# Forward segment in another order: V before Q and among turns and scores, out-projection in two parts

## The chip, the cores and the metric

One NeuronCore of a Trainium2 chip. The metric is the device time of one execution in microseconds (us). Runs of the kernel before took 2990.2, 2992.72 and 2992.77 us, median 2992.72 us. The traces come from one further execution of each kernel under the hardware profiler.

## The reference

A transformer block with a recurrent memory, and its gradients. The change touches the forward attention alone:

```python
B, S, Dm = (1, 2048, 512)
H, Dh = (32, 128)
M, seg = (8, 32)
...
for s in range(n_seg):
    xs = x[:, s * seg_len:(s + 1) * seg_len, :].copy()
    h = jnp.concatenate([mem, xs], axis=1)
    q = jnp.einsum('btd,dhe->bhte', h, Wq)
    k = jnp.einsum('btd,dhe->bhte', h, Wk)
    v = jnp.einsum('btd,dhe->bhte', h, Wv)
    scores = jnp.einsum('bhqe,bhke->bhqk', q, k) * scale
    scores = jnp.where(mask[None, None], scores, -1000000000.0)
    p = _softmax(scores, axis=-1)
    o = jnp.einsum('bhqk,bhke->bhqe', p, v)
    o = jnp.einsum('bhte,hed->btd', o, Wo)
    mem = o[:, :M, :].copy()
    outs.append(o[:, M:, :])
```

There are 64 segments of 32 rows. Each takes the 8 memory rows that the segment before put out, so 40 rows stand in front of the projections and the segments run strictly one after the other. Around this the reference has a layernorm with conditioning, a gated feed-forward block, and the gradients of all weights; those stages are the same in both kernels.

## The kernel before

The forward is `phase2`, a Python loop `for s in range(NS)` that writes out 64 segments. `pin` then fixes each engine's instructions in the order in which the program states them, so the source order is the order of every engine. Four segments make a tile of 128 rows; `s4 = s % 4` is a segment's place in it.

A segment does the following, in this order. The names are those of the profile.

- K and Q: `proj` calls `col_pass` (L257), 32 columns of TensorE at a time, four such column groups side by side, two halves for each of K and Q. VectorE copies the first half from PSUM to `RA`, ScalarE the second. `RA` holds heads in rows of four.
- V in three chunks: `v_chunk` (L673), twice 512 columns and once 384, again in 32-column groups. The first two carry rows of the tile after (`hb`, the last 8 rows of each segment) in the fourth group. Their copies go to `Vst` and `RBv`.
- Turns (`turns`, L851): eight 128x128 transposes each of k and q, and copies by `to_heads` into `kT` (ScalarE) and `qT` (VectorE). `to_heads` has an own part (three of four heads, in two halves of 4) and a far part (the heads of the fourth row group, two instructions).
- Scores (`st_exp`, L861) in three parts of 4, 4 and 3 head groups, each group three heads of 40 rows, then an exp on ScalarE into `ET`.
- Column sums (`den`, L867), reciprocals on VectorE, products with V (`pv`, L887) into `or_ps`, and `ost`, which scales the result into `Ost`: parts 0 and 2 on VectorE (L911), part 1 on ScalarE in four instructions.
- Turns of O (`ott`, through `transposes_part`, L879) and copies into `OT`.
- Out-projection (`outproj`, `pair_mm` L223): 16 pairs of heads, each four matmuls of 32 columns, all into one PSUM tile `at_ps`.
- The fold: `split_pair` makes a high part (ScalarE `at_hi`) and a low part (VectorE `at_lo`), `sum_pair` adds them on TensorE (`at_ft`, L242), and ScalarE writes the new memory rows into the `hT` of the next segment (L1058), for which its K waits.

Other work stands between these: `p1` is the layernorm of a later tile in five steps (0 load of x on SP's queue, 1 statistics, 2 scaling, 3 shift and a store by POOL, 4 turn on TensorE); `fill` issues pieces of the next tile's last-8-rows projections and turns (`b_pieces`); `tail.chunk` the out-projection of such rows (L215); `pop_later` a postponed fold or turn of rows that go to DRAM. The queue of SP (SyncE) carries the loads and stores in program order: stores of `RA` (`rows_out`), two transposing transfers (`VTr` from `Vst`, `Pst` from `ET`), stores of `Ost` and `OT`. POOL multiplies `Pst` by the reciprocals (L1076, in `norm`), copies the last-8-row columns into `kT` and `qT` (`tails_in`), and issues the transfers of `v_tails`.

PSUM tiles of the forward come from one pool of 5 buffers with the tag "p" and one of 3 for the scores; a new tile waits until the buffer that it gets has been read out.

```python
                    v_chunk(s, 0)
                    turns()
                    v_chunk(s, 1)
...
                st_exp(0)
                st_exp(1)
                st_exp(2)
```

Of the kernel before, what the change touches and what calls it, by code (L numbers as in the profile page):

```python
# [40 lines left out]
class K:  # L41
# [403 lines left out]
    def phase2(self):  # L445
# [15 lines left out]
        with ExitStack() as ctx:  # L461
# [234 lines left out]
            def v_chunk(s, k):  # L696
# [4 lines left out]
                ps = psp.tile([128, 512], F32, name="pass_ps", tag="p")  # L701
                hT = get_ht(s)
                for c in range(DC):
# [4 lines left out]
                if k > 0:  # L708
                    v_evac(("dve", "act")[k - 1], Vsts[s % 2], ps, a, n)
                for hl, ta, tn, o in tails_of:  # L710
                    self.evac(("act", "dve")[k], RBv[(t + 1) % 2][32 * hl:32 * hl + 32, ta * E:(ta + tn) * E],
                              ps[96:128, o * E:(o + tn) * E])
                if k == 0:
                    v_evac("dve", Vsts[s % 2], ps, a, n)
# [109 lines left out]
            for s in range(NS):  # L824
                s4 = s % nseg_t
                if s4 == 0:
                    if s > 0:
                        p1(s // nseg_t + P1_AHEAD, 0)
# [18 lines left out]
                def turns(xs=(("k", "act"), ("q", "dve"))):  # L847
                    for x, eng in xs:
                        tp = psp.tile([128, 8, 128], BF16, name="turn_ps", tag="p")
                        for i in range(8):  # L850
                            nc.tensor.transpose(tp[:, i, :], RA[x][:, i * 128:i * 128 + 128], self.ident[:, :])  # L851
                        for hf in range(2):
                            to_heads(eng, XT[x], tp[:, 4 * hf:4 * hf + 4, :], 4 * hf, 4, 32, 0, far=False)
                        to_heads(eng, XT[x], tp[:], 0, 8, 32, 0, own=False)

                def st_exp(pi):
                    st_ps = masked.pop(pi)
                    n = min(PG, G - pi * PG)
                    for j in range(n):
                        g = pi * PG + j  # L860
                        nc.tensor.matmul(st_ps[:, j, 0:120], lhsT=x120(KT, g), rhs=QT[:, g * 120:g * 120 + 120],  # L861
# [52 lines left out]
                def ott(pi):  # L914
                    ps, n = transposes_part(Ost, pi, m=120)
                    self.evac("dve" if pi == 0 else "act", part3(OT, pi)[:, 0:n, 0:120], ps)

                def outproj():
                    ps = psp.tile([128, 256], F32, name="at_ps", tag="p")
                    off = lambda h: (h // 3) * GW + (h % 3) * 32  # L920
                    order = [*range(12, 16), *range(8, 12), *range(8)] if s == 0 else range(H // 2)
                    for n, p in enumerate(order):
                        hs = (2 * p, 2 * p + 1)
# [17 lines left out]
                if s == 0:  # L941
# [6 lines left out]
                    turns((("k", "act"),))  # L948
# [1495 lines left out]
```

## Time and profile before

| | before |
|---|---|
| median of the runs shown | 2992.72 us |
| the profiled execution | 2989.77 us |
| its span, first to last instruction | 2988.0 us |
| TensorE matmul busy | 2907.6 us, 97% |
| VectorE / ScalarE / POOL busy | 55% / 45% / 41% |
| forward: first K matmul of segments 0 and 63 | 18.3 us, 950.0 us |
| granted TensorE clock | 0.996 |

The span is the time from the first to the last instruction of one execution. Busy TensorE is not TensorE at its peak: a matmul's record includes its passage through the array, and records overlap. In lists in order of time the first column is the start and the second the duration of the merged row in us; then engine, line, operation, the tile written and the tiles read, shape, and how many instructions were merged. What stands in brackets is idle time ahead of the row and what ended it. "PE" is TensorE, "PEld" its weight load, "DVE" VectorE, "ACT" ScalarE.

### The profile page before, as it was taken

The page shows a single profiled execution, that of the slowest core. Times are in us where ns is not written, and L with a number is a line of the kernel's source. Part 1 is how long each engine was busy: PE and PEld are TensorE (multiplying, and loading weights), DVE is VectorE, ACT ScalarE, POOL GpSimd, SP SyncE. Part 2 cuts the span into 40 slices and gives each one's busy share as a digit, 9 for nine tenths or more (in the row PEclk, how much of TensorE's full clock was granted, in tenths as well). Part 3 has the DMA queues.
Part 4 walks back from the last instruction along what each step waited for, and adds up shares of the span by engine and source line. Part 5 has one row for each costly group of instructions (what it writes and reads, how often), then busy time and mean ns, then how long its engine had stood idle before and what let it go on. Part 6 is the DMA issues. An engine that isn't in the chain of part 4 may idle for free.

```text
span 2988.0 us, 105331 instructions
## 1 busy us (share of the span) xinstructions
PE 2907.6 (97%) x43742; PEld 1825.2 (61%) x43816; DVE 1639.3 (55%) x3680; ACT 1347.5 (45%) x3244; POOL 1228.8 (41%) x2485
## 2 busy tenths in 40 slices
PE   6999999999999999999999999999999999999999
PEld 3666666666666544446567777777777754445455
DVE  5566656666655788833356666656566632850011
ACT  3666666666666533312355555555555520110011
POOL 2455555544555222221244444444444422762111
PEclk8999999999999999999999999999999999999999
DMA  9998988888889899988699999999999997886565
GB/s 308 212 229 216 214 210 225 205 218 216 211 217 267 219 232 231 232 274 284 191 256 255 250 256 246 257 253 252 251 247 252 246 283 246 252 262 191 159 216 171
DMA packets 837922, 703.01 MB, mean 235 GB/s; under 512 B 537682, under 2 KB 709890, under 8 KB 836548
## 3 DMA queue, kind: packets, MB, share of 16 engines
q1 hardware_dynamic: 711828, 485.29, 65.9%
q0 software_dynamic: 54512, 148.63, 15.8%
q10 hardware_dynamic: 71104, 62.34, 6.5%
q8 instruction: 345, 5.65, 0.8%
q14 instruction: 133, 1.09, 0.1%
HBM read 294.99 MB, written 276.35 MB: 191 GB/s over the span
## 4 chain that ended last, share of the span: by engine, by line
PE 68%; DMA 2%; DVE 1%; ACT 1%; issue 1%; POOL 0%; SPq 0%; DVEq 0%; ACTq 0%; POOLq 0%
PE gps L2225 14%; PE dh_ps L215 8%; PE pass_ps L257 7%; PE g_ps L1848 5%; PE gps5o L2240 4%; PE dhq_ps L223 4%; PE mm L1329 3%; PE dh_tps L215 3%; PE gps L1508 3%; PE mm L1289 2%; PE mm L1304 2%; PE tps L1765 2%; PE mm L1258 1%; PE mm L1262 1%; PE turn_ps L1721 1%; PE gps L1407 1%
## 5 line engine op out<-in xcount | busy, mean ns | idle before, releaser
L2225 PE MATMUL gps<-rows,hrows 128*128 128x512 bf16 (+2 forms) x2124 | 413.6, 355 | 1.9
L2225 PEld LDWEIGHTS <-hrows 128*128 128x128 bf16 x2160 | 211.1, 98 | 204.5 <-issue 0.9
L63 DVE CAST ot<-gps 128x512 bf16<-128x512 f32 (+3 forms) x76 | 48.2, 634 | 309.2 <-PE gps L2225 229.1
L1076 POOL TENSOR_TENSOR Pst<-Pst,rden 120x1408 bf16<-120x1408 bf16 x63 | 159.7, 2536 | 132.4 <-issue 84.2
L61 ACT ACTIVATE ot<-gps 128x512 bf16<-128x512 f32 (+3 forms) x75 | 41.2, 549 | 349.5 <-PE gps L2225 214.8
L1893 POOL COPY dOst<-RAd 96x512 bf16<-96x512 bf16 x128 | 75.3, 611 | 298.7 <-DVE RAd L63 298.5
L673 PE MATMUL pass_ps<-Wv,hT 128*32 128x512 bf16 (+2 forms) x2304 | 186.7, 358 | 0.0
L2229 POOL DMA_DIRECT2D out_dram<-ot x104 | 78.5, 755 | 254.8 <-DVE ot L63 129.2
L257 PEld LDWEIGHTS <-hT 128*32 128x32 bf16 x4096 | 114.7, 97 | 98.5 <-issue 4.4
L223 PE MATMUL at_ps<-Wo,OT 128*32 128x256 bf16 x4096 | 125.9, 276 | 10.6 <-ACT OT L61 5.5
L215 PE MATMUL dh_ps<-WvT,dVT 128*32 128x512 bf16 x2048 | 134.0, 381 | 1.6
L63 DVE CAST Vst<-pass_ps 96x512 bf16<-96x512 f32 x128 | 87.2, 682 | 84.8 <-ACT RBv L61 76.2
L673 PE MATMUL pass_ps<-Wv,hb 128*32 128x512 bf16 (+2 forms) x636 | 127.5, 348 | 2.1 <-DMA Wv<-in_A_Wv_dram 2.1
L257 PE MATMUL pass_ps<-Wk,hT 128*32 128x512 bf16 x2048 | 123.4, 382 | 2.5 <-DVE mv L402 1.1
L257 PE MATMUL pass_ps<-WoT,dyT 128*32 128x256 bf16 (+1 forms) x3072 | 122.5, 308 | 1.1 <-ACT dyT L1974 0.9
L223 PE MATMUL dhq_ps<-WqT,dQT 128*32 128x256 bf16 x4096 | 123.1, 273 | 0.0
L257 PE MATMUL pass_ps<-Wq,hT 128*32 128x512 bf16 x2048 | 122.7, 379 | 0.0
L215 PE MATMUL dh_ps<-WkT,dKT 128*32 128x512 bf16 x2048 | 122.3, 380 | 0.0
L2240 PE MATMUL gps5o<-WoT,rows 128*128 128x512 bf16 x549 | 120.4, 379 | 0.6
L223 PEld LDWEIGHTS <-OT 128*32 128x32 bf16 x4096 | 107.8, 97 | 21.4 <-issue 12.7
L814 POOL DMA_DIRECT2D Vst<-RBv x192 | 100.3, 527 | 48.5 <-ACT ET L863 31.2
L223 PEld LDWEIGHTS <-dQT 128*32 128x32 bf16 x4096 | 109.8, 97 | 15.9 <-issue 0.2
(473 smaller groups left out, 6989.4 us busy)
## 6 DMA issues: line engine op xcount, KB each, us to landing
OSR<-Ost SPq DMA_DIRECT2D x64, 352.0 KB
OT<-OT SPq DMA_DIRECT2D x64, 352.0 KB
PS<-Pst SPq DMA_DIRECT2D x64, 352.0 KB
Pst_l<-PS SPq DMA_DIRECT2D x64, 352.0 KB
OT_l<-OT SPq DMA_DIRECT2D x64, 352.0 KB
DVR<-rows_x POOLq DMA_DIRECT2D x64, 352.0 KB, 6.3
DKR<-rows_x POOLq DMA_DIRECT2D x64, 352.0 KB, 5.8
DQR<-rows_x POOLq DMA_DIRECT2D x64, 352.0 KB, 3.2
```

The lines of the kernel that those rows point to most:

```text
L63: return nc.vector.tensor_copy(out, in_)
L215: self.nc.tensor.matmul(ps[32 * j:32 * j + 32, :], lhsT=lhsT, rhs=w, start=(n < 4), stop=(n >= total - 4), tile_position=(0, 32 * j))
L223: nc.tensor.matmul(ps[32 * j:32 * j + 32, :], lhsT=x[k], rhs=w[k][:, 256 * d:256 * d + 256], start=(n == 0), stop=(n == total - 1), tile_p ...
L257: self.nc.tensor.matmul(ps[32 * j:32 * j + 32, :], lhsT=lhs(c), rhs=rhs, start=(c == 0), stop=(c == DC - 1), tile_position=(0, 32 * j))
L673: nc.tensor.matmul(ps[32 * j:32 * j + 32, o * E:(o + n) * E], lhsT=lhsT, rhs=wc[:, 3 * a + hl:3 * (a + n - 1) + hl + 1:3, :], start=(c == ...
L814: nc.gpsimd.dma_start(Vst[96 + 8 * j:104 + 8 * j, :], rb[32 * j + o:32 * j + o + 8, :])
L1076: nc.gpsimd.tensor_tensor(Pst[0:120, :, :], Pst[0:120, :, :], rden[:, :].unsqueeze(2).to_broadcast([120, G, 128]), op=ALU.mult)
L1329: nc.tensor.matmul(hp[:], lhsT=xT[:, fc, :], rhs=wT[:, fc, :], start=(n == 0), stop=(n == 2 * FC - 1))
L1508: nc.tensor.matmul(ps[:], lhsT=h2r[:, j, c * 128:(c + 1) * 128], rhs=xr[:, j, :], start=(j == 0), stop=(j == NT - 1))
L1848: nc.tensor.matmul(ps[:, j, 0:w], lhsT=lh[:, g * GW:(g + 1) * GW], rhs=rh[:, g * GW:g * GW + w], start=True, stop=True)
L2225: nc.tensor.matmul(ps[:, 0:ng * E], lhsT=hrows[:, tp_, c * 128:(c + 1) * 128], rhs=rows[:, tp_, 0:ng * E], start=(tp_ == 0), stop=(tp_ == ...
L2240: nc.tensor.matmul(pss[gg][:], lhsT=rows[:, t, gg * E:(gg + 1) * E], rhs=dyrows[:, t, :], start=(n == 0), stop=(n == NTP - 1))
```

## The change

K is followed by V's first chunk, then Q. The turns of q come in two halves, and V's second chunk in two halves by rows of the contraction (`v_products` with `cs`), so that the order on TensorE is: turns of k, first half of q's turns, half of V1, second half of q's turns, scores part 0, rest of V1, scores part 1, half of V2, scores part 2, rest of V2. The copies stand in the order in which the scores need them, and k's far copies go from ScalarE to VectorE. The last score group of parts 0 and 1 reads 120 columns of `KT` in place of 128. Ahead of the last part of `pv` stand the fill of turns and `p1` step 4. The turn of O's part 0 and its copy come before the last `ost`; parts 1 and 2 share one PSUM tile, and part 2's copy goes from ScalarE to VectorE. The first 6 pairs of the out-projection run between the turns of parts 1 and 2. The steps of `p1` are spread over other segments (load and statistics at s4 = 2, scaling at s4 = 3, shift at s4 = 0, turn at s4 = 1).

```diff
--- before.py
+++ after.py
@@ -693,25 +693,31 @@
                             v_mm(ps, j, c, hb_rows(0)(c), j, a, n)
                     v_evac("dve", RBv[0], ps, a, n)
 
-            def v_chunk(s, k):
+            def v_products(s, k, ps, cs):
 
                 t, s4 = s // nseg_t, s % nseg_t
                 a, n = VCH[k]
                 tails_of = VTAILS.get((s4, k), ()) if t + 1 < NT else ()
-                ps = psp.tile([128, 512], F32, name="pass_ps", tag="p")
+                ps = ps or psp.tile([128, 512], F32, name="pass_ps", tag="p")
                 hT = get_ht(s)
-                for c in range(DC):
+                for c in cs:
                     for j in range(3):
                         v_mm(ps, j, c, hT[:, c, :], j, a, n)
                     for of in tails_of:
                         v_mm(ps, 3, c, hb_rows(t + 1)(c), *of)
-                if k > 0:
-                    v_evac(("dve", "act")[k - 1], Vsts[s % 2], ps, a, n)
-                for hl, ta, tn, o in tails_of:
+                return ps
+
+            def v_copies(s, k, ps):
+
+                t, s4 = s // nseg_t, s % nseg_t
+                a, n = VCH[k]
+                v_evac(("dve", "dve", "act")[k], Vsts[s % 2], ps, a, n)
+                for hl, ta, tn, o in VTAILS.get((s4, k), ()) if t + 1 < NT else ():
                     self.evac(("act", "dve")[k], RBv[(t + 1) % 2][32 * hl:32 * hl + 32, ta * E:(ta + tn) * E],
                               ps[96:128, o * E:(o + tn) * E])
-                if k == 0:
-                    v_evac("dve", Vsts[s % 2], ps, a, n)
+
+            def v_chunk(s, k):
+                v_copies(s, k, v_products(s, k, None, range(DC)))
 
             def fill(s4, where):
                 for f in slots.pop((s4, where), []):
@@ -823,9 +829,9 @@
 
             for s in range(NS):
                 s4 = s % nseg_t
+                if s4 == 2:
+                    p1(s // nseg_t + P1_AHEAD + 1, 0)
                 if s4 == 0:
-                    if s > 0:
-                        p1(s // nseg_t + P1_AHEAD, 0)
                     slots = b_pieces(s // nseg_t + 1) if s + nseg_t < NS else {}
                 hT = get_ht(s)
                 hT_next = get_ht(s + 1) if s + 1 < NS else None
@@ -844,21 +850,31 @@
                     for x in "kq":
                         rows_out(RA[x], DR[x], s, 1)
 
-                def turns(xs=(("k", "act"), ("q", "dve"))):
-                    for x, eng in xs:
-                        tp = psp.tile([128, 8, 128], BF16, name="turn_ps", tag="p")
-                        for i in range(8):
-                            nc.tensor.transpose(tp[:, i, :], RA[x][:, i * 128:i * 128 + 128], self.ident[:, :])
-                        for hf in range(2):
-                            to_heads(eng, XT[x], tp[:, 4 * hf:4 * hf + 4, :], 4 * hf, 4, 32, 0, far=False)
-                        to_heads(eng, XT[x], tp[:], 0, 8, 32, 0, own=False)
+                def turn_mm(x, tp, hf):
+                    tp = tp or psp.tile([128, 8, 128], BF16, name="turn_ps", tag="p")
+                    for i in range(4 * hf, 4 * hf + 4):
+                        nc.tensor.transpose(tp[:, i, :], RA[x][:, i * 128:i * 128 + 128], self.ident[:, :])
+                    return tp
+
+                def turn_own(x, tp, hf, eng):
+                    to_heads(eng, XT[x], tp[:, 4 * hf:4 * hf + 4, :], 4 * hf, 4, 32, 0, far=False)
+
+                def turn_far(x, tp, eng):
+                    to_heads(eng, XT[x], tp[:], 0, 8, 32, 0, own=False)
+
+                def turns(x, eng):
+                    tp = turn_mm(x, turn_mm(x, None, 0), 1)
+                    turn_own(x, tp, 0, eng)
+                    turn_own(x, tp, 1, eng)
+                    turn_far(x, tp, eng)
 
                 def st_exp(pi):
                     st_ps = masked.pop(pi)
                     n = min(PG, G - pi * PG)
                     for j in range(n):
                         g = pi * PG + j
-                        nc.tensor.matmul(st_ps[:, j, 0:120], lhsT=x120(KT, g), rhs=QT[:, g * 120:g * 120 + 120],
+                        w = 120 if g in (PG - 1, 2 * PG - 1) else 128
+                        nc.tensor.matmul(st_ps[0:w, j, 0:120], lhsT=KT[:, g * 120:g * 120 + w], rhs=QT[:, g * 120:g * 120 + 120],
                                          start=False, stop=True, skip_group_check=True)
                     nc.scalar.activation(part3(ET, pi)[:, 0:n, 0:120], st_ps[:, 0:n, 0:120], AF.Exp, scale=cfg.scale)
 
@@ -911,16 +927,29 @@
                     nc.vector.tensor_tensor(part3(Ost, pi)[0:120, 0:n, :], or_ps[0:120, 0:n, :],
                                             rden[:, pi * PG:pi * PG + n].unsqueeze(2).to_broadcast([120, n, 128]), op=ALU.mult)
 
-                def ott(pi):
-                    ps, n = transposes_part(Ost, pi, m=120)
-                    self.evac("dve" if pi == 0 else "act", part3(OT, pi)[:, 0:n, 0:120], ps)
-
-                def outproj():
-                    ps = psp.tile([128, 256], F32, name="at_ps", tag="p")
+                def ott_first():
+                    ps, n = transposes_part(Ost, 0, m=120)
+                    self.evac("dve", part3(OT, 0)[:, 0:n, 0:120], ps)
+
+                def ott_rest():
+                    ps = psp.tile([128, 2 * PG, GW], BF16, name="tps", tag="p")
+                    for pi in (1, 2):
+                        n = min(PG, G - pi * PG)
+                        for j in range(n):
+                            g = pi * PG + j
+                            nc.tensor.transpose(ps[:, g - PG, 0:120], Ost[0:120, g * GW:(g + 1) * GW],
+                                                self.ident[0:120, 0:120])
+                        self.evac(("act", "dve")[pi - 1], part3(OT, pi)[:, 0:n, 0:120], ps[:, (pi - 1) * PG:(pi - 1) * PG + n, 0:120])
+                        if pi == 1:
+                            yield
+                    yield
+
+                def outproj(ps, a, b):
+                    ps = ps or psp.tile([128, 256], F32, name="at_ps", tag="p")
                     off = lambda h: (h // 3) * GW + (h % 3) * 32
                     order = [*range(12, 16), *range(8, 12), *range(8)] if s == 0 else range(H // 2)
-                    for n, p in enumerate(order):
-                        hs = (2 * p, 2 * p + 1)
+                    for n in range(a, b):
+                        hs = (2 * order[n], 2 * order[n] + 1)
                         self.pair_mm(ps, [OT[:, off(h):off(h) + 32] for h in hs], [Wo[:, h, :] for h in hs], n, H // 2)
                     return ps
 
@@ -945,7 +974,7 @@
                     load_wo(0)
                     for f in firsts["k"]:
                         f()
-                    turns((("k", "act"),))
+                    turns("k", "act")
                     evac_turned()
                     tails_in("k", 0)
                     p1(1, 4)
@@ -960,36 +989,46 @@
                         firsts["q"][hf]()
                         proj("q", hf, ("dve", "act")[hf])
                     firsts["q"][2]()
-                    turns((("q", "dve"),))
+                    turns("q", "dve")
                     evac_turned()
                     tails_in("q", 0)
                     for f in first_stores:
                         f()
                 else:
+                    v_chunk(s, 0)
                     proj("q", 0, "dve")
-                    if s4 == 1:
-                        p1(s // nseg_t + P1_AHEAD, 2)
                     proj("q", 1, "act")
                 if s == NS - 1:
                     first_tile[4]()
                 if s > 0:
-                    v_chunk(s, 0)
-                    turns()
-                    v_chunk(s, 1)
+                    tk = turn_mm("k", turn_mm("k", None, 0), 1)
+                    tq = turn_mm("q", None, 0)
+                    turn_own("k", tk, 0, "act")
+                    turn_own("k", tk, 1, "act")
+                    turn_own("q", tq, 0, "dve")
+                    v1 = v_products(s, 1, None, range(0, DC // 2))
+                    turn_mm("q", tq, 1)
+                    turn_own("q", tq, 1, "dve")
+                    turn_far("k", tk, "dve")
+                    turn_far("q", tq, "dve")
+                st_exp(0)
+                if s > 0:
+                    v_products(s, 1, v1, range(DC // 2, DC))
+                    v_copies(s, 1, v1)
+                st_exp(1)
+                if s > 0:
+                    v2 = v_products(s, 2, None, range(0, DC // 2))
+                st_exp(2)
+                if s > 0:
+                    v_products(s, 2, v2, range(DC // 2, DC))
+                    v_copies(s, 2, v2)
                 if s == NS - 1:
-                    v_chunk(s, 2)
                     first_tile[5]()
-                if s == NS - 1:
                     late_rows()
                     self.glu_first = {1: self.glu_load(1, nc.sync)}
-                st_exp(0)
-                st_exp(1)
-                st_exp(2)
-                if s == NS - 1:
                     turn_v(0)
                     turn_v(1)
                 if 0 < s < NS - 1:
-                    v_chunk(s, 2)
                     v_tails(s + 1)
                 if s < NS - 1:
                     nc.sync.dma_start(VTr[:], Vst[:, :], transpose=True)
@@ -1007,34 +1046,36 @@
                 ost(0, or0, "dve")
                 ost(1, or1, "act")
                 den(2, or2)
-                early = s4 == 0 and len(self.later) > 1
+                fill(s4, "turn")
+                if s == 3 or s4 == 1 and s > 1:
+                    p1(s // nseg_t + P1_AHEAD, 4, evacs)
                 pv(2, or2)
                 recip(2, 3, or2)
-                ost(2, or2, "dve")
-                fill(s4, "turn")
-                if s4 == 2:
-                    p1(s // nseg_t + P1_AHEAD, 4, evacs)
                 if s == NS - 1:
                     turn_v(2)
-                ott(0)
+                ott_first()
+                ost(2, or2, "dve")
                 if s4 == 3:
                     tail.chunk()
-                if early:
+                if s4 == 0 and len(self.later) > 1:
                     self.pop_later()
-                ott(1)
-                ott(2)
-                if not early:
-                    self.pop_later()
+                rest = ott_rest()
+                next(rest)
+                at_ps = outproj(None, 0, 6) if s > 0 else None
+                next(rest)
+                self.pop_later()
                 self.pop_later()
                 if s == NS - 1:
                     nc.gpsimd.dma_start(self.w_down, io["B_w_down"].rearrange("(fc p) d -> p fc d", p=128))
                     for g0, t, w in ((0, RAs[0]["k"], 8), (8, RAs[0]["q"], G - 8)):
                         nc.sync.dma_start(self.VT[s, :, g0:g0 + w, :], t[:, 0:w * GW].rearrange("p (g x) -> p g x", x=GW))
                 nc.sync.dma_start(self.OSR[s], gl3(Ost))
-                at_ps = outproj()
+                at_ps = outproj(at_ps, 6 if s > 0 else 0, H // 2)
                 evac_turned()
-                if s4 < 2:
-                    p1(s // nseg_t + P1_AHEAD, (1, 3)[s4])
+                if s < 3:
+                    p1(P1_AHEAD, s + 1)
+                if s4 != 1 and s > 0:
+                    p1(s // nseg_t + P1_AHEAD + (s4 > 0), {2: 1, 3: 2, 0: 3}[s4])
                 if NS - 4 <= s < NS - 1:
                     first_tile[s - NS + 4]()
                 elif s == NS - 1:
```

## Prediction

> **What bounds the kernel now.** I read the page first (busy shares, then the chain that ended last), then what TensorE waited for in the stretch from 100 to 960 us, then TensorE's own order of time over single segments.
>
> ```profile
> span 2988.0 us, 105331 instructions
> ...
> PE 2907.6 (97%) x43742; PEld 1825.2 (61%) x43816; DVE 1639.3 (55%) x3680; ACT 1347.5 (45%) x3244; POOL 1228.8 (41%) x2485
> ...
> PE 68%; DMA 2%; DVE 1%; ACT 1%; issue 1%; POOL 0%; SPq 0%; DVEq 0%; ACTq 0%; POOLq 0%
> ```
>
> TensorE (PE) is the bound; nothing else holds more than 2% of the chain. The change touches the forward alone: 64 segments one behind the other, from 18 to about 964 us. So the question is how many microseconds of idle TensorE the new order removes, and how many it costs to issue. The waits that the profile names there:
>
> ```profile
> PE tps L879 <- DVE Ost L911: 11.7, 31, 0.4
> PE st_ps L861 <- DVE qT L63: 4.6, 11, 1.6
> PE at_ps L223 <- ACT OT L61: 4.5, 13, 0.4
> PE at_ps L223 <- DVE at_rb L341: 4.4, 14, 0.3
> PE at_ft L242 <- ACT at_hi L230: 2.0, 4, 0.5
> ```
>
> The columns are microseconds in all, times, and the longest. All of it is under 30 us, and these are the waits that the change aims at. They understate a little, since a matmul's record runs on after the next could have started; so below I go by starts. One segment whole (the first of a tile of four):
>
> ```profile
> 506.10 1.91 PE L257 MATMUL pass_ps<-Wk,hT 128*32 128x512 bf16 x32
> 507.82 1.91 PE L257 MATMUL pass_ps<-Wq,hT 128*32 128x512 bf16 x32
> ...
> 510.53 0.62 PE L851 MATMUL turn_ps<-ident,RA0k 128*128 128x128 bf16 x8
> 510.99 0.61 PE L851 MATMUL turn_ps<-ident,RA0q 128*128 128x128 bf16 x8
> 511.53 0.40 PE L673 MATMUL pass_ps<-Wv,hT 128*32 128x512 bf16 x3
> ...
> 511.97 0.39 PE L673 MATMUL pass_ps<-Wv,hT 128*32 128x512 bf16 x3
> ...
> 512.19 0.39 PE L673 MATMUL pass_ps<-Wv,hT 128*32 128x512 bf16 x3
> ...
> 512.51 0.75 PE L861 MATMUL st_ps<-qT,kT 128*128 128x120 bf16 x11
> 513.19 0.83 PE L673 MATMUL pass_ps<-Wv,hT 128*32 128x384 bf16 x12
> 513.95 0.37 PE L867 MATMUL or_ps<-ones,ET 128*128 128x1 bf16 x8
> ...
> 515.47 0.39 PE L879 MATMUL tps<-ident,Ost 120*128 120x120 bf16 x4 [0.38 <-DVE Ost L911]
> ...
> 516.47 1.93 PE L223 MATMUL at_ps<-Wo,OT 128*32 128x256 bf16 x64
> 518.23 1.04 PE L257 MATMUL pass_ps<-Wk,hb 128*32 128x512 bf16 x16
> ```
>
> Two prices lie in these starts. **A switch.** Groups of four 32-column matmuls (form 128*32) start 0.22 apart (511.97, 512.19), but from the last group to the scores (form 128*128) it is 0.32: 0.10 more. The eight turns of k take 0.46 (510.53 to 510.99), the eight of q up to the next 32-column group 0.54: 0.08 to 0.09 more. So leaving the 32-column form and coming back costs TensorE 0.19 us. The same two sums stand, within 0.02, at almost every such place of the forward. The Trainium skill says in "TensorEngine Tiling (Array Packing)", Key Properties, that changing the tiling mode drains TensorE; the trace agrees with 0.10 and 0.09 us. **A wait.** From the first column sums (513.95) to the turns of O (515.47) is 1.52, of which 0.55 is TensorE waiting for VectorE's Ost.
>
> I call the four segments of a tile kinds 0 to 3 (s4 in the code). From the first K matmul to the next segment's, kinds 0 to 3 take 13.90, 14.17, 14.52 and 14.83 us (starts 506.10, 520.00, 534.17, 548.69, 563.52).
>
> **The change, part by part**, in us after a segment's first K matmul.
>
> *More switches.* Same matmuls, same number (the built orders have equally many TensorE rows). Before, a segment has 32-column stretches broken by: turns, scores, sums to turns of O, the fold (at_ft). After, V1 and V2 are each cut in half, with the second half of q's turns and scores part 0, then part 1, then part 2 between, and the out-projection is cut in two by the last turns of O. That is three more breaks: 3 x 0.19 = 0.57 us, in 63 segments 36 us. It lies beside nothing: it is TensorE's own time.
>
> *Front half.* Without waits the sums (L867) start at 7.85 (kinds 0 and 2). Kind 1 is at 8.16 and kind 3 at 8.02: scores waited for qT, which was behind other copies on VectorE. In the new order q's own copies stand ahead of all else, and the scores need only their own part: the first copy ends at about 5.66 and the second at 6.49, against scores at 5.95 and 6.75. So these waits go (0.31 in kind 1, 0.17 in kind 3), and two of the three switches come: the sums start at 7.85 + 0.38 = 8.23 in every kind. The four far copies and V1's follow on VectorE and end at about 8.4, before the reciprocal at 8.6: hidden; k's two leave ScalarE, which is not waited for.
>
> *Turns of O.* The reorder leaves the chain sums, reciprocal, Ost on VectorE: 1.50 to 1.52 from sums to first turn in kinds 0, 2 and 3, 1.44 in kind 1. So turns start at 9.72 in each kind. The turn of a tile (p1tp, 0.22) moves from kind 2 to kind 1, under this wait.
>
> *Out-projection in two.* Its first part needs OT part 0. VectorE now copies it before the last Ost: the four turns take 0.16 to the last start, that one ends 0.22 later, copy 0.40 (row "OT<-tps 128x480"), hand-overs 0.05 to 0.07 each: 0.90 after 9.72, so 10.62. ScalarE's four Ost copies end 2.0 after the sums (10.23), so their turns are done in time. Six pairs of 0.108 (1.73 over 16) and a switch: last turns at 11.37; three turns, the late turn of at, a switch: second part at 11.68, ten pairs, end at 12.76. Kind 0 has one small turn more (12.82). Kind 3 has eight tail matmuls (0.43 and a switch each way) between, so its OT is in time: 13.0. Before, the out-projection ended at 12.13, 12.41, 12.74 and 13.05. **Sum: +0.69, +0.35, +0.02, -0.05.** Kinds 2 and 3 gain back a wait of 0.42 ahead of the out-projection (560.00 against 559.46 + 0.15 in kind 3), because the last turns now share one PSUM tile.
>
> *Work moved on VectorE.* The layernorm steps of a later tile move: statistics from kind 0 to kind 2, scaling (two instructions) from kind 1 to kind 3, both ahead of at_lo in VectorE's order. Behind at_lo waits the second fold matmul, and behind that the next segment's hT. Kind 2: statistics take 1.09 (516.72 to 517.81), from 12.55 to 13.64; at_lo ends at 14.03, wanted at 13.84: +0.2. Kind 3: the scaling starts at about 12.8:
>
> ```profile
> L411 DVE TENSOR_SCALAR xh<-x,mv,rstd x16: 538/1468/2884, 7.0 to 811.6; 128x512 f32<-128x512 bf16 x16
> ```
>
> Smallest, median, largest duration: it took 0.54 in the first segments, and 1.47 or more wherever POOL's 2.54 us product Pst (L1076) was running, ending 0.3 after that. At its new place POOL runs copies of 0.20 to 0.35. So 0.54 + 0.69 (L412): at_lo ends at 14.43, wanted at 14.09: +0.35 (bounds: 0 if VectorE gets there sooner, +1.3 if it takes 1.47 again). The Trainium skill, "SBUF — State Buffer", says VectorE and GpSimd take a shared port pair by an exclusive lock for a whole instruction; L411 beside L1076 agrees; by it the scaling could wait for one POOL copy, inside these bounds. Thirteen tiles have these steps.
>
> *Queues.* The load of x goes from kind 0 to kind 2, at the head of SP's queue there (about 1 us of issue). Pst<-ET is issued at 546.31 in kind 2, POOL needs it 5.4 later, and the next scores' exp later still: nothing.
>
> **Sum.** 63 segments are 15.75 of each kind: 15.75 x (0.69 + 0.35 + 0.02 - 0.05) = 15.9; 13 x (0.2 + 0.35) = 7.2; together **+23 us**. The profiled execution took 2989.8 us (span 2988.0 and 1.8 around it), so 3012.8; the median of the runs shown is 2992.7, 2.9 above it, so **3016 us**. Bounds of the steps: 0.1 per segment either way in the hand-overs (6 us), 0 to 1.3 in kind 3 (-5 to +12), 0 to 0.4 in kind 2 (3): 3002 to 3034.
>
> **Rivals.**
> 1. *A switch costs nothing where nothing is waited for.* The step up to the 128-column form always stands before an instruction with a semaphore wait in the trace; the new ones may be free where that wait is long over. Then 0.57 a segment falls away: 23 - 36 = -13, so 2980. It decides below 23 / (3 x 63) = 0.12 off each of the 189 pairs, that is under 0.07 for a pair. For: the waits. Against: the step down (turns to V1) has no other engine's wait and costs 0.09, and the amounts do not vary.
> 2. *Half of it:* only the step up is free, 189 x 0.10 = 19 less: +4, 2997, no change that can be told.
> 3. *The late at_lo is worse:* scaling at 1.47 beside POOL, at_lo 0.9 later in 13 segments (+12), and the hand-overs at their upper end: 3032. For: 11 of the 16 durations. Against: POOL's product runs at the start of a segment, not at its end.
>
> **Chances.** Forecast 0.55 (own range 3004 to 3026), rival 3 0.19, rival 2 0.14, rival 1 0.12. A measurement here tells about 0.2%, 6 us. Faster: rival 1 nearly whole, 0.11. Same: most of rival 2, 0.13. Slower: 0.76. The range 2992 to 3034 leaves out rival 1, the lower edge of rival 2 and the end of rival 3.
>
> **What would show it.** After: scores in three stretches, each with 0.10 before and 0.09 behind it; sums at about 8.2 with no wait for qT; tps still waiting for Ost, about 0.5 in kind 0; a new wait of at_ps for VectorE's OT, 0.2 to 0.3; no wait for at_rb; at_ft waiting for at_lo in kinds 2 and 3. Kinds 0 to 3 at about 14.6, 14.5, 14.7 and 15.1. I am wrong if the new switches show no extra time, if the turns of O start sooner than 1.4 behind the sums, or if the segments shorten.

## Result and profile after

| | before | after |
|---|---|---|
| median of the runs beside one another | 2991.46 us (2988.51 to 2992.77) | 3025.38 us (3021.75 to 3027.05) |
| ratio, with its 95% interval | | 1.0107 [1.0092, 1.0121] |
| the profiled execution, its span | 2989.77 us, 2988.0 us | 3024.85 us, 3023.0 us |
| first K matmul of segments 0 and 63 | 18.3 us, 950.0 us | 19.4 us, 979.7 us |
| granted TensorE clock | 0.996 | 0.998 |

The change makes the kernel 34 us slower, 1.07%. Of the 35.0 us between the two spans, 1.1 lie ahead of the first segment, 28.6 between the first K matmuls of segments 0 and 63, and 5.3 behind that.

The page of the changed kernel, busy time and the chain that ended last:

```profile
span 3023.0 us, 105372 instructions
...
PE 2949.0 (98%) x43816; PEld 1800.7 (60%) x43816; DVE 1672.0 (55%) x3870; ACT 1315.5 (44%) x3054; POOL 1233.6 (41%) x2485
...
PE 62%; DMA 2%; ACT 1%; DVE 1%; issue 1%; POOL 0%; SPq 0%; DVEq 0%; ACTq 0%; POOLq 0%
```

TensorE was busy 41.4 us longer on the same matmuls (both traces have 43816 weight loads; that of before lacks 74 of the matmul records), and the rest of the span shrank from 80.4 to 74.0 us. So the loss isn't in waits that the profile names; it sits inside what the profile counts as busy. What TensorE still waits for from 100 to 990 us of the changed kernel (us in all, times, longest):

```profile
PE tps L895 <- DVE Ost L927: 9.0, 31, 0.4
PE at_ps L223 <- DVE OT L63: 5.1, 31, 0.2
PE at_ft L242 <- DVE at_lo L232: 3.5, 16, 0.5
PE at_ft L242 <- ACT at_hi L230: 2.0, 4, 0.5
```

The waits for qT (4.6), at_rb (4.4) and ScalarE's OT (4.5) are gone. In their place stand the out-projection waiting for OT's first copy on VectorE, and the second fold waiting for at_lo.

One segment of kind 0 on the changed kernel's TensorE, in order of time (start, duration, what stands behind it):

```profile
524.88 0.39 PE L856 MATMUL turn_ps<-ident,RA0q 128*128 128x128 bf16 x4
525.20 0.40 PE L673 MATMUL pass_ps<-Wv,hT 128*32 128x512 bf16 x3
...
525.43 0.39 PE L673 MATMUL pass_ps<-Wv,hT 128*32 128x512 bf16 x3
...
525.75 0.40 PE L856 MATMUL turn_ps<-ident,RA0q 128*128 128x128 bf16 x4
525.98 0.38 PE L877 MATMUL st_ps<-qT,kT 128*128 128x120 bf16 x4
526.29 0.40 PE L673 MATMUL pass_ps<-Wv,hT 128*32 128x512 bf16 x3
...
526.52 0.39 PE L673 MATMUL pass_ps<-Wv,hT 128*32 128x512 bf16 x3
...
526.84 0.39 PE L877 MATMUL st_ps<-qT,kT 128*128 128x120 bf16 x4
527.15 0.50 PE L673 MATMUL pass_ps<-Wv,hT 128*32 128x384 bf16 x6
527.59 0.33 PE L877 MATMUL st_ps<-qT,kT 128*128 128x120 bf16 x3
527.85 0.50 PE L673 MATMUL pass_ps<-Wv,hT 128*32 128x384 bf16 x6
528.28 0.35 PE L883 MATMUL or_ps<-ones,ET 128*128 128x1 bf16 x8
...
529.79 0.38 PE L895 MATMUL tps<-ident,Ost 120*128 120x120 bf16 x4 [0.38 <-DVE Ost L927]
...
530.73 0.84 PE L223 MATMUL at_ps<-Wo,OT 128*32 128x256 bf16 x24
531.50 0.33 PE L940 MATMUL tps<-ident,Ost 120*128 120x120 bf16 x3
531.67 0.22 PE L339 MATMUL at_tp<-ident,at_tb 128*128 128x128 bf16 x1
531.73 0.22 PE L339 MATMUL ao_b_tp<-ident,ao_b_tb 128*128 128x128 bf16 x1
```

The scores stand in three stretches and nothing in front of them carries a wait in brackets. From the last 32-column group to the 128-column form it is 0.32 each time (525.43 to 525.75, 526.52 to 526.84), where groups of one form follow at 0.23. Between 524.88 and 528.28 no row has a bracket, and TensorE still needs more time than before for the same matmuls. Brackets show idle time from about 0.15 us up, so a shorter wait would not be seen there; the experiment with one more break below settles that.

Over many segments: medians over segments 12 to 51 of starts in the two traces, in us after the segment's first K matmul.

| | kind 0 | kind 1 | kind 2 | kind 3 |
|---|---|---|---|---|
| column sums, before | 7.85 | 8.29 | 7.85 | 8.03 |
| column sums, after (predicted 8.23) | 8.29 | 8.29 | 8.29 | 8.31 |
| turns of O, after (9.72) | 9.80 | 9.79 | 9.80 | 9.82 |
| out-projection begins, after (10.62) | 10.73 | 10.73 | 10.74 | 10.99 |
| second fold behind the first, before | 0.15 | 0.15 | 0.15 | 0.15 |
| second fold behind the first, after | 0.15 | 0.15 | 0.25 | 0.45 |
| whole segment, before | 13.90 | 14.30 | 14.51 | 14.83 |
| whole segment, after (14.6, 14.5, 14.7, 15.1) | 14.75 | 14.69 | 14.79 | 15.24 |

The four kinds together grew by 1.93 us, which over 15.75 segments of each is 30.4 us. In kinds 0 and 2, where the scores had no wait before, the column sums come 0.44 later (8.29 for 7.85), with two breaks more ahead of them.

### The profile page after: what moved, and what is told of

It reads as the page before. It is cut to its first block, busy times and chain, and to the rows that moved or that the text cites. A ratio compares the mean times of both kernels' runs of the same rounds, so it can differ in the third digit from the quotient of the medians.

```text
span 3023.0 us, 105372 instructions
## 1 busy us (share of the span) xinstructions
PE 2949.0 (98%) x43816; PEld 1800.7 (60%) x43816; DVE 1672.0 (55%) x3870; ACT 1315.5 (44%) x3054; POOL 1233.6 (41%) x2485
## 4 chain that ended last, share of the span: by engine, by line
PE 62%; DMA 2%; ACT 1%; DVE 1%; issue 1%; POOL 0%; SPq 0%; DVEq 0%; ACTq 0%; POOLq 0%
PE gps L2266 14%; PE dh_ps L215 8%; PE g_ps L1889 5%; PE pass_ps L257 5%; PE gps5o L2281 4%; PE dhq_ps L223 4%; PE mm L1370 3%; PE gps L1549 3%; PE dh_tps L215 3%; PE mm L1330 2%; PE mm L1345 2%; PE tps L1806 2%; PE mm L1299 1%; PE mm L1303 1%; PE gps L1448 1%; PE dp_ps L1866 1%
## 5 line engine op out<-in xcount | busy, mean ns | idle before, releaser
L673 PE MATMUL pass_ps<-Wv,hT 128*32 128x512 bf16 (+2 forms) x2304 | 209.0, 359 | 0.0
L345 POOL DMA_DIRECT2D AOA<-at_rb x64 | 36.8, 574 | 342.9 <-DVE at_rb L341 243.3
L223 PE MATMUL at_ps<-Wo,OT 128*32 128x256 bf16 x4096 | 136.8, 276 | 8.0 <-DVE OT L63 5.8
L673 PE MATMUL pass_ps<-Wv,hb 128*32 128x512 bf16 (+2 forms) x636 | 137.7, 349 | 1.4 <-DMA Wv<-in_A_Wv_dram 1.4
L879 ACT ACTIVATE ET<-st_ps 128x480 bf16<-128x480 f32 (+1 forms) x192 | 102.2, 537 | 61.2 <-ACT kT L61 29.6
```

The costliest lines, as they stand in the source:

```text
L223: nc.tensor.matmul(ps[32 * j:32 * j + 32, :], lhsT=x[k], rhs=w[k][:, 256 * d:256 * d + 256], start=(n == 0), stop=(n == total - 1), tile_p ...
L673: nc.tensor.matmul(ps[32 * j:32 * j + 32, o * E:(o + n) * E], lhsT=lhsT, rhs=wc[:, 3 * a + hl:3 * (a + n - 1) + hl + 1:3, :], start=(c == ...
L879: nc.scalar.activation(part3(ET, pi)[:, 0:n, 0:120], st_ps[:, 0:n, 0:120], AF.Exp, scale=cfg.scale)
```

## The experiments

Each kernel ran beside the kernel before on the same chip; ratios are to that. "Kinds" are medians as in the table above.

**V whole again.** After, with V1, V2 and q's turns undivided:

```diff
-                    tq = turn_mm("q", None, 0)
+                    tq = turn_mm("q", turn_mm("q", None, 0), 1)
...
-                    v1 = v_products(s, 1, None, range(0, DC // 2))
-                    turn_mm("q", tq, 1)
                     turn_own("q", tq, 1, "dve")
+                    v1 = v_products(s, 1, None, range(DC))
...
-                    v_products(s, 1, v1, range(DC // 2, DC))
...
-                    v2 = v_products(s, 2, None, range(0, DC // 2))
...
-                    v_products(s, 2, v2, range(DC // 2, DC))
-                    v_copies(s, 2, v2)
+                    v_chunk(s, 2)
```

> The changed kernel with V's chunks 1 and 2 and the turns of q whole again (no scores between halves); order of copies, out-projection in two parts and moved steps as in the change. Theory A (each break of a 32-column stretch costs TensorE 0.19 us whether or not anything is waited for): two breaks fewer in 63 segments, 2 x 0.19 x 63 = 24 us less than the changed kernel's 3025: 3001 us, column sums at 7.9 after a segment's first K matmul in place of 8.29, and still no wait of the scores for qT, since q's own copies stay first. Theory B (the break is free where nothing is waited for; the lost time is later copies and the late at_lo): within 5 us of 3025.

Measured: 3005.85 us, 1.0044 [1.0029, 1.0059], near the first theory's 3001. Column sums at 7.95 in every kind instead of 8.29, kinds 14.43, 14.37, 14.47, 14.91. So the cuts of V and q's turns cost 0.34 a segment net, and 20 us in the time. Against the kernel before, q's turns end 0.10 later (5.38 for 5.28): with V ahead of Q they wait for ScalarE's copy of Q's second half. With q's turns divided, that wait was hidden. The two breaks themselves therefore cost 0.34 + 0.10 = 0.44, or 0.22 each, which is what kinds 0 and 2 show in the table above.

**Out-projection whole again**, with the turns of O as before (last Ost first, three PSUM tiles), V still in halves:

```diff
-                at_ps = outproj(None, 0, 6) if s > 0 else None
...
-                at_ps = outproj(at_ps, 6 if s > 0 else 0, H // 2)
+                at_ps = outproj(None, 0, H // 2)
```

> The changed kernel with turns of O and out-projection as before the change (three PSUM tiles, the last Ost ahead of the first turn, all 16 pairs together); all else as in the change. Theory A: one break fewer (12 us) and no wait of at_ps for VectorE's OT (0.18 in three of four segments, 8 us), but kinds 1 to 3 get back a wait for a PSUM tile (about 0.4 in each, 19 us): 3015 to 3028 us, kind 0 shorter by 0.4 and kinds 1 to 3 about as long as in the changed kernel. Theory B (the split itself is what costs, through OT and the shared tile): 3005 or less, all four kinds shorter by 0.3.

Measured: 3020.21 us, 1.0098 [1.0079, 1.0118]; kinds 14.32, 14.80, 14.80, 15.29. The first theory had this. Kind 0 is 0.43 shorter than after, and the other kinds are 0.01 to 0.11 longer, because the wait ahead of the out-projection is back there (it begins at 11.28 in kinds 1 and 2). The cut buys nothing by keeping TensorE busy: in kinds 1 to 3 its break and its wait for OT cost about as much as the wait that it goes around. The shared PSUM tile went with the cut here; further on it stands without one.

**Layernorm steps back** where they stood before, the rest as after:

```diff
                     proj("q", 0, "dve")
+                    if s4 == 1:
+                        p1(s // nseg_t + P1_AHEAD, 2)
                     proj("q", 1, "act")
...
-                if s == 3 or s4 == 1 and s > 1:
+                if s4 == 2:
                     p1(s // nseg_t + P1_AHEAD, 4, evacs)
```

> The changed kernel with the layernorm steps of later tiles at their places of before. Theory A: the waits for at_lo in kinds 2 and 3 go (0.10 and 0.30 in 13 tiles, 5 us), but the turn of a tile is exposed again in kind 2 (0.2) and the scaling beside POOL's product takes 1.47 us and holds q's copies in kind 1 (0.2): within 5 us of 3025. Theory B (the moved steps are a main part of the loss): 3015 or less.

Measured: 3037.53 us, 1.0155 [1.0139, 1.0171]: slower than after by 12, which neither theory had. Kind 1 takes 16.13 instead of 14.69; kind 3 gains 0.29. In 12 tiles that is 14 us; the two traces differ by 16.6 between segments 0 and 63. VectorE in one segment of kind 1 of this kernel, in order of time:

```profile
547.12 0.69 DVE L63 CAST RA1q<-pass_ps 128x512 bf16<-128x512 f32 x1 [0.18 <-PE pass_ps L257]
547.72 1.94 DVE L411 TENSOR_SCALAR xh<-x,mv,rstd 128x512 f32<-128x512 bf16 x1
549.70 0.69 DVE L412 TENSOR_TENSOR xh<-xh,ca_bc 128x512 f32<-128x512 f32 x1
550.30 0.35 DVE L63 COPY qT<-turn_ps 128x384 bf16<-128x384 bf16 x1
```

POOL at that time:

```profile
546.82 2.55 POOL L1117 TENSOR_TENSOR Pst<-Pst,rden 120x1408 bf16<-120x1408 bf16 x1
```

And TensorE:

```profile
550.71 0.38 PE L856 MATMUL turn_ps<-ident,RA1q 128*128 128x128 bf16 x4 [1.46 <-DVE qT L63]
```

The scaling takes 1.94 and ends at 549.66, 0.29 behind POOL's product (549.37). The copy just ahead of it, out of PSUM, runs beside the same product at its usual 0.69. Behind the scaling stands q's first copy, and behind that the second half of q's turns, which writes the PSUM tile that this copy reads: TensorE stands for 1.46. Before, a scaling of 1.47 or more at this place cost kind 1 less: its column sums come at 8.29 where they come at 7.85 in the run with the steps alone, below, so 0.44 (0.31 in the tile that the prediction read). There q's turns were one piece, and all of V1 lay between them and the scores. With divided turns the first copy is wanted sooner, so the moved scaling repairs what the cut would have broken.

**One more break**, where nothing is waited for: the small turns (L339) go into the second part of the out-projection, five pairs after its start:

```diff
-                at_ps = outproj(at_ps, 6 if s > 0 else 0, H // 2)
+                at_ps = outproj(at_ps, 6 if s > 0 else 0, 11)
+                if s > 0:
+                    self.pop_later()
+                    self.pop_later()
+                at_ps = outproj(at_ps, 11, H // 2)
```

> The changed kernel with one more break: the late turn of at (one 128-column transpose or two, whose operand is long ready) moves from the break before the out-projection's second part to the middle of that part. Nothing else changes, no wait is added. Theory A: 0.19 us more in each of 63 segments, 12 us: 3037, and in the trace 0.10 ahead of the turn and 0.09 behind it. Theory B (a break without a wait is free): 3025.

Measured: 3044.3 us, 1.0175 [1.016, 1.019]; kinds 14.97, 14.91, 15.29, 15.74. TensorE there:

```profile
529.26 0.33 PE L940 MATMUL tps<-ident,Ost 120*128 120x120 bf16 x3
529.51 0.73 PE L223 MATMUL at_ps<-Wo,OT 128*32 128x256 bf16 x20
530.17 0.23 PE L339 MATMUL at_tp<-ident,at_tb 128*128 128x128 bf16 x1
530.33 0.73 PE L223 MATMUL at_ps<-Wo,OT 128*32 128x256 bf16 x20
```

Five pairs at 0.108 are 0.54, but the next row starts 0.66 behind: 0.12 for the step up. The single turn, 0.05 to 0.06 elsewhere, holds 0.16: 0.10 for the step down. No bracket stands at either, and the trace's semaphores show no shorter wait: in segments 12 to 51 the turn either waits for none or for one that was set 0.58 before it starts, and the matmul behind it waits for none. In every kind the out-projection ends 0.22 later. Kinds 0 and 1 grow by just that. Kinds 2 and 3 grow by 0.50, because at_rb's copy, now late, stands on VectorE ahead of the statistics, the scaling and at_lo: a cost that was not foreseen, and the reason why the time came out above both theories.

**No cut left**: V as in the first experiment and the out-projection as in the second.

> After with V1, V2 and q's turns in one piece each, the out-projection in one piece, and the turns of O as before (last Ost first, three PSUM tiles). What is left of the change: V's first chunk in front of Q, the copies in another order, the layernorm steps in other segments. No cut is left. A (the cuts make the loss, the rest is small): column sums at about 7.95, kinds about 14.0, 14.4, 14.5 and 15.0, time 2994 to 3003. B (the order of the copies or the moved steps cost by themselves, 10 us or more): 3008 or more.

Measured: 3000.46 us, 1.0033 [1.002, 1.0046]; column sums 7.95, kinds 14.00, 14.48, 14.48, 14.96. First theory: 25 of the 34 us are the cuts, net of what they gain. Of the other 9, the kinds show 0.37 together, 6 us, and V in front of Q alone is 0.10 in each kind; what makes the last 3 is not shown.

**No cuts, but the shared PSUM tile** for the last turns of O, and the steps at better places (statistics at the end of kind 0, scaling of kind 1, shift of kind 2):

```diff
-                ott(1)
-                ott(2)
+                ott((1, 2))
...
+                if s4 < 3 and s > 3:
+                    p1(s // nseg_t + P1_AHEAD + 1, s4 + 1)
```

> After without any cut: V1, V2, q's turns and the out-projection whole, last Ost before the first turns of O; kept are the shared PSUM tile of the last turns of O, the copy of part 2 on VectorE and the steps in other segments; scaling goes to the end of kind 1, shift to kind 2. A (the break is the price, and the shared PSUM tile and the moved scaling are gains that the cuts ate): column sums at 7.95 in all kinds, out-projection from about 10.4, kinds 14.0, 14.1, 14.1 and 14.4, so 14 to 20 us below before: 2970 to 2980. B (the gains exist only together with the cut out-projection, which keeps TensorE busy while OT is copied): the out-projection waits 0.3 or more for OT in all kinds, time 2990 or more.

Measured: 2987.98 us, 0.9993 [0.9983, 1.0002]; kinds 14.07, 14.09, 14.31, 14.46. No change that can be told: 3 us below before, where the first theory expected 14 to 20. The second theory's wait for OT, 0.3 or more, is not there either: the out-projection begins at 10.47, 10.55, 10.72 and 10.87, where the run before it had 10.47, 10.96, 10.96 and 11.44. So, with the shared tile and the steps at these places, the wait that the cut out-projection was to fill goes without a cut. By the kinds the gain would be 0.61 x 15.75 = 10 us; kind 2 had been put 0.2 too low, and the rest is the uncertainty between kinds and times that is taken up below.

**The same with Q ahead of V again.**

```diff
-                    v_chunk(s, 0)
                     proj("q", 0, "dve")
                     proj("q", 1, "act")
+                    v_chunk(s, 0)
```

> The same without cuts, but Q stands ahead of V's first chunk again, as before. A (V in front of Q makes q's turns wait 0.10 us for ScalarE's copy of Q's second half, with nothing gained from it): q's turns end at 5.28 instead of 5.38, every kind 0.10 shorter, 63 x 0.10 = 6 us below the variant with V first, so about 2964 to 2974. B (V first brings something for the copies on VectorE, which are else late for the scores): the scores wait for qT, equal or up to 10 us above it.

Measured: 3019.18 us, 1.01 [1.0085, 1.0115]; kinds 14.61, 14.63, 14.86, 15.20. q's turns do end at 5.28 again, but the last scores come at 7.61 instead of 7.05: the second theory, at three times its price. ScalarE of this kernel in one segment of kind 0, in order of time:

```profile
523.86 0.59 ACT L61 ACTIVATE RBv<-pass_ps 32x512 bf16<-32x512 f32 x1 [1.01 <-DVE Vst L63]
524.47 0.87 ACT L61 ACTIVATE kT<-turn_ps 128x384 bf16<-128x384 bf16 x2
```

VectorE there:

```profile
523.14 0.69 DVE L63 CAST Vst<-pass_ps 96x512 bf16<-96x512 f32 x1 [1.06 <-PE pass_ps L673]
524.10 0.62 DVE L63 COPY qT<-turn_ps 128x384 bf16<-128x384 bf16 x2 [0.28 <-PE turn_ps L856]
525.38 0.36 DVE L63 COPY kT<-turn_ps 128x192 bf16<-128x192 bf16 x2 [0.65 <-ACT kT L61]
525.65 0.35 DVE L63 COPY qT<-turn_ps 128x192 bf16<-128x192 bf16 x2
```

TensorE there:

```profile
526.05 0.33 PE L877 MATMUL st_ps<-qT,kT 128*128 128x120 bf16 x3 [0.27 <-DVE qT L63]
```

The chain reads upwards: the scores wait for q's far copy, which stands behind k's far copy on VectorE; that waits for k's own copies on ScalarE, which stand behind V0's copy into RBv, which waits for VectorE's copy of the same PSUM tile. In front of Q, V0's two copies are done before the turns. So the parts of the change hang together: with k's far copies on VectorE and V0's copies in their new order, V in front of Q is needed, and it costs 0.10.

**The steps alone**, on the kernel before, at the places that the change gives them:

```diff
-                if s4 < 2:
-                    p1(s // nseg_t + P1_AHEAD, (1, 3)[s4])
+                if s < 3:
+                    p1(P1_AHEAD, s + 1)
+                if s4 != 1 and s > 0:
+                    p1(s // nseg_t + P1_AHEAD + (s4 > 0), {2: 1, 3: 2, 0: 3}[s4])
```

> The kernel before with one part of the change alone: the layernorm steps in other segments (load and statistics in kind 2, scaling in kind 3, shift in kind 0, turn in kind 1). A (they gain the wait for qT in kind 1, 0.31, and lose 0.10 in kind 2 and 0.30 in kind 3): kinds 13.9, 14.0 to 14.2, 14.5 and 15.1, time within 5 us of before: 2987 to 2997. B (the steps are the costly part of the change): 3000 or more.

Measured: 2989.95 us, 1.0002 [0.9993, 1.0011]; kinds 13.90, 14.37, 14.15, 14.97. No change, as the first theory had it, but kinds 1 and 2 came out otherwise. In kind 1 the scores come 0.34 earlier (6.41 for 6.75), and the out-projection begins at 10.85 where it began at 10.78. TensorE in that kind:

```profile
526.47 1.01 PE L879 MATMUL tps<-ident,Ost 120*128 120x120 bf16 x11 [0.16 <-DVE Ost L911]
...
527.95 1.93 PE L223 MATMUL at_ps<-Wo,OT 128*32 128x256 bf16 x64 [0.28 <-ACT OT L61]
```

The wait for qT is gone and a wait ahead of the out-projection has taken its place. Kind 2 gains 0.36, where nothing was expected: without the turn of the tile its out-projection begins at 10.37 in place of 10.99 (medians), and the late at_lo takes back part of it, the second fold following 0.41 behind the first. The out-projection in one segment of kind 2, before and then here:

```profile
545.17 1.93 PE L223 MATMUL at_ps<-Wo,OT 128*32 128x256 bf16 x64 [0.35 <-ACT OT L61]
```

```profile
541.85 1.93 PE L223 MATMUL at_ps<-Wo,OT 128*32 128x256 bf16 x64
```

**Steps and shared tile on the kernel before**, with its own order of V and copies; steps as in the variant with the shared tile above. **And the shared tile alone.** Both have the `ott` edit shown there.

> The kernel before, order of copies and V as it was, with two things of the change: the last turns of O in one shared PSUM tile (part 2's copy on VectorE), and the layernorm steps moved, scaling to the end of kind 1 and shift to the end of kind 2. A (these two are what the change had to give, its cuts and its order of copies only cost): scores at 6.41 in kinds 0 to 2, out-projection from 10.4, 10.5, 10.6 and 10.9, kinds 13.97, 14.0, 14.2 and 14.5, sum 56.7 against 57.54 before, so 0.87 x 15.75 = 14 us less: 2974 to 2982. B (moving work off the early stretch brings nothing, since another wait takes its place before the out-projection, as in kind 1 of the run with the steps alone): within 5 us of before.

> The kernel before with the shared PSUM tile of the last turns of O alone. A (it takes the wait of the out-projection's tile away in kinds 2 and 3, 0.24 and 0.39, and costs 0.07 in each kind, since VectorE copies part 2 a little later than ScalarE did): kinds 13.97, 14.37, 14.34 and 14.51, 5 us below before: 2983 to 2989. B (the wait was for VectorE's and ScalarE's own work, not for a tile): kinds 2 and 3 as before, 2990 to 2998.

Measured: both parts 2980.45 us, 0.9967 [0.9954, 0.998], kinds 14.01, 13.96, 13.96, 14.52; the tile alone 2982.84 us, 0.9975 [0.9965, 0.9986], kinds 13.96, 14.39, 14.03, 14.52. The first has the lowest median of the study, 10 us below before and 45 below after, though its interval overlaps that of the tile alone; the expectation of 2974 to 2982 held. The tile alone came out just below what was expected, with 0.48 gained in kind 2 where 0.17 was expected net. Kind 1 shows the two waits covering each other: 14.37 with the steps alone, 14.39 with the tile alone, 13.96 with both. Whether the tile or the copy of part 2 on VectorE does it was not separated.

**After, with only the steps at the better places:**

> After with every cut kept, and only the layernorm steps placed as in the two fastest variants (statistics at the end of kind 0, scaling at the end of kind 1, shift at the end of kind 2). A (the late low part of at, 0.10 in kind 2 and 0.30 in kind 3, is a loss of its own beside the cuts): the second fold follows the first by 0.15 in all kinds, kinds 14.75, 14.7, 14.7 and 14.95, 15.75 x 0.40 = 6 us below after: 3015 to 3022. B (the late low part is only moved to the kind in which the steps now run): kind 1 longer by 0.3, time as after, 3023 to 3028.

Measured: 3019.07 us, 1.01 [1.0083, 1.0117]; kinds 14.75, 14.69, 14.70, 14.95, second fold 0.15 behind the first in all. First theory: the late at_lo was a loss of its own, 0.09 and 0.29, some 5 us in the 12 tiles that show it; the median is 6 below after.

## Why the prediction came out right

It forecast 3016 us with an own range to 3026; the median is 3025.4, just inside. The mechanism was right and its largest term too small: of a loss of 34 us it had 23. That the total stayed in the range owes something to luck, since two terms were too large the other way. By its own steps:

- **Breaks: three per segment, 0.19 each.** The number and the places were right, the price was not: 0.22, by the run with V whole (two breaks, 0.44) and the one with a break more (0.22). The prediction read 0.10 for the step up and 0.08 to 0.09 down; the runs show 0.12 and 0.10. Three breaks in 63 segments are 41.6 us and not 36: 5.7 of the miss. The column sums at 8.29 for 8.23 are the same error. The Trainium skill, "TensorEngine Tiling (Array Packing)", Key Properties, says that a change of tiling mode drains TensorE; these runs agree in that the change costs time, 0.22 us there and back.
- **Waits removed.** qT's wait went in kinds 1 and 3 as predicted, and at_rb's. Sums now come at the same time in every kind. The prediction put the gain ahead of the out-projection in kinds 2 and 3 down to the shared PSUM tile; in kind 2 the moved turn of the tile does it too, by the run with the steps alone.
- **Turns of O and hand-overs.** Sums to turns 1.51 (1.49 said), turns to out-projection 0.93 (0.90 said): 3 us together.
- **Kind 1 before.** The prediction read it from one tile, 14.17; the median is 14.30. That alone made its loss 0.13 x 15.75 = 2 us too large.
- **Late at_lo.** +0.10 and +0.30, where +0.2 and +0.35 stood: in the 12 tiles that show them 4.8 us, against 7.2. VectorE in a segment of kind 3 of the changed kernel:

```profile
577.16 0.54 DVE L411 TENSOR_SCALAR xh<-x,mv,rstd 128x512 f32<-128x512 bf16 x1
577.73 0.71 DVE L412 TENSOR_TENSOR xh<-xh,ca_bc 128x512 f32<-128x512 f32 x1
578.36 0.41 DVE L232 TENSOR_TENSOR at_lo<-at_ps,at_hi 128x256 bf16<-128x256 f32 x1
```

TensorE at the same place:

```profile
578.38 0.27 PE L242 MATMUL at_ft<-foldsel,at_hi 128*128 128x32 bf16 x4
578.83 0.27 PE L242 MATMUL at_ft<-foldsel,at_lo 128*128 128x32 bf16 x4 [0.18 <-DVE at_lo L232]
```

at_lo begins when the scaling's two instructions are through, 0.02 before the first fold, and the second fold follows 0.45 behind the first.

The corrected terms give 23.1 + 5.7 + 3 - 2 - 2.4 = 27 us for the forward; the two traces show 28.6 between segments 0 and 63, and the medians of the kinds 30.4, which leave out single segments such as 1 and 13, shorter after by 1.52 and 0.90. The remaining 5 to 6 us of the difference are not assigned. The first K matmul of segment 0 stands anywhere from 18.2 to 19.7 in the traces of this study, and what comes after segment 63's first K, untouched by the change, takes 2038 us in the trace of before, 2043 in that of after and up to 2045 in the others, so one execution of each cannot place it.

The rivals: a break that is free where nothing is waited for (2980), or only half paid (2997), fell with the run with one more break: 0.12 and 0.10 without any wait. The third, 3032 by a scaling of 1.47 beside POOL, fell as a mechanism, though its time was closer (6.6 us off, the forecast 9.4): the scaling takes 0.54 at its new place. Its fact was right, only elsewhere: where the scaling stays beside POOL's product, the new order loses 1.44 in each kind 1.

## What to carry to other kernels

Cutting matmuls of one form into pieces to fill waits costs TensorE a change of form there and back, here 0.22 us, and the profile counts it as busy: compare starts with the time that the same matmuls took undivided, and cut only for a wait longer than that. A wait that goes can bring out a second one right behind it; two edits that gain nothing alone can gain together (0.34 in kind 1 here), so try them together before dropping either. Before a step moves on an in-order engine, look at what then stands behind it and at what runs beside it on the other engines.

## What the runs showed of the hardware that was not expected

The scaling (L411, 128x512 bf16 to f32) takes 0.54 with no POOL product beside it. Beside POOL's 2.55 us product it takes 1.47 to 1.97, and once 2.88, longer the earlier it starts, and ends 0.3 behind the product each time. Once, with the steps back, it started 0.28 ahead of the product and kept its 0.54. A copy of the same size out of PSUM, started beside the same product, keeps its 0.69. The Trainium skill, "SBUF — State Buffer", Terms, says that VectorE and GpSimd arbitrate for a shared port pair, which one instruction holds exclusively to its end while the loser blocks. The scaling agrees with it. The copy shows that not every VectorE instruction is held up; it differs from the scaling both in reading PSUM and in its operation, and no run here separates the two.
